# A planner's table of instruction-fetch times and a price for bank marks, with the order of a fused attention and feed-forward kernel searched anew

## The chip, the cores and the metric

The kernel runs on one core of a Trainium2 chip. The metric is the device time of one execution in microseconds (us). Five engines of the core work side by side and wait for one another by semaphores: TensorE (PE; its weight loads are listed apart as PEld), VectorE (DVE), ScalarE (ACT), GpSimd (POOL) and SyncE (SP), the last of which mostly issues transfers (DMA).

## The reference

Decayed attention without a softmax, then a feed-forward block whose gate is h cos(h). There are 8 batches of 8 heads, 576 positions and a head width of 64, so 4608 tokens of width 512; the feed-forward width is 2048.

```python
scores = scale * np.matmul(q, k.transpose(0, 1, 3, 2))
gamma = 1.0 - 2.0 ** (-5.0 - np.arange(H))
Dmat = np.where(rel >= 0, gamma[:, None, None] ** rel[None, :, :], 0.0)
x = np.matmul(scores * Dmat, v)             # then (B*S, H*D)
h = x @ w_in
out = (h * np.cos(h)) @ w_out
```

## The kernel before, in words

**Work and tiles.** Attention is computed in chunks of 64 positions with a running state of each head. A unit `(b, g)` is 256 positions of batch b (g 0 or 1) or the last 64 positions of four batches (g 2). For each unit, K, Q and V are loaded by SP, cast or weighted to bf16 (`unit`, L549 and L599), and transposed on TensorE (`tpe`, L623) or by a transposing transfer (`txb`). The scores, states and outputs are narrow matmuls on quarters of the 128x128 array (64x64 tiles); `emit_lanes` collects them in tasks whose names begin with "ses", and all run from L669. Two units make a token block of 512; there are nine. The first product of a block is either sixteen plain tiles (`mlp1`, L878) or, for blocks 4 to 8, a Strassen-like form with seven products in place of eight (`seven1`, L1007). The second product always has the seven-product form (`wino2`, L1147). These are wide matmuls on the full array.

**Banks and marks.** PSUM has eight banks of 512 columns (pool `bk`). A product that continues on a copied first product has its bank seeded by ScalarE (`seed`, L938). The bank must be "whole" for that, as its last write left it; where it isn't, `emit` (L451) first issues a mark (`mark`, L486, the matmul at L487), a matmul of ones over the bank. Places that may need one are the seeds of `seven1` and `wino2`.

**The planner.** The order isn't written by hand. `graph` builds the tasks of all engines with their durations, dependences and buffers. `prios` gives each a priority, `shift` moves priorities by a table `SHIFT` (text: an index step and a shift within some 40 us, in tens of ns), and `run` (L242) schedules: at each step it takes, over the engines, the task that can start first, among nearly equal ones that with the best priority. It keeps an instruction counter `seen` for TensorE, two for each matmul. Instructions come to TensorE in blocks of 256; `run` notes when the block k is asked for (instruction 128+256k, `asked`) and, in `pick`, delays a task that passes instruction 443+256k until that time plus `fetch(asked)` (L187). So `fetch`, a step function of the time of the run, decides how closely tasks with many small matmuls follow one another in the plan. The times exist in the plan only: the chip runs the order found. The choice of a bank prefers a whole one for a seed (L340). Where the plan has a gap on TensorE, `emit` adds filler matmuls (`warm`, L490, matmul at L493), which keep the array busy at the start.

The `SHIFT` table was found by a search outside the kernel, whose result alone stands in it.

Of the kernel before, what the change touches and what calls it, by code (L numbers as in the profile page):

```python
# [11 lines left out]
B, H, S, D = 8, 8, 576, 64  # L12
# [4 lines left out]
TB = 512  # L17
# [105 lines left out]
def lat(a, b):  # L123
    if a.dma:
        return 60
    if a.eng == b.eng:
        return 285 if a.then is b else 0 if a.eng == "pe" else 60
    return LAT[a.eng]


class Graph:
# [53 lines left out]

    @staticmethod
    def fetch(at):  # L187
        return 11500 if at < 30000 else 10000 if at < 55000 else 8500 if at < 100000 else 7200 if at < 205000 else 6200

    ENTER, LEAVE, BOND = 95, 105, 2000  # L190

    def switch(self, one, two):
# [49 lines left out]
    def run(self):  # L242
        self.reset()
        free = {e: 0.0 for e in ("pe", "act", "dve", "pool", "sp")}
        ready = {e: [] for e in free}
        seen, asked, whole = 20, {}, [False] * 8
        dma_free, port_free = 0.0, {"dve": 0.0, "pool": 0.0}
        est, order, last, mode, held = {}, [], None, "", None
# [53 lines left out]
        n = 0  # L302
        while n < len(self.tasks):
            best = None
            for e in free:
                c = pick(e)
                if c and (best is None or c[0] < best[0]):
                    best = c
            if best is None:
                rest = [(t.name, t.eng, [b.pool for b in t.allocs]) for e in ready for t in ready[e]]  # L310
                keep = {p: [b and [(t.name, t.eng) for t in b.tasks if t.start is None] for b in h] for p, h in self.holder.items()}
                raise RuntimeError(f"the scheduler is stuck: {self.pools} {free} {[x for x in rest if x[0][:3] == 'ses']} {rest[:12]} {keep}")
            s, t = best
            e = t.eng
            if e == "pe":
                s = max(s, free[e] + self.switch(mode, t.name))
            gap = s - free["pe"]
            ready[e].remove(t)
            t.start, t.order = s, n
            n += 1  # L320
            free[e] = s + t.dur
            if t.port:
                port_free[e] = s + t.dur
                if e == "dve":
                    last = t
                elif last and last.start > s - self.SINCE:
                    t.parts[0][4]["push"] = last
            if e == "pe":
                mode = t.name
                held = t.then or (held if t is not held else None)  # L330
                if gap > 400 and s < 40000:
                    seen += 2 * max(1, self.fill(gap, s - gap))
                k = (seen + t.count - 128) // 256
                if k >= 0 and k not in asked:
                    asked[k] = s + t.dur * max(0, 128 + 256 * k - seen) / max(1, t.count)
                seen += t.count
            for b in t.allocs:
                pool = self.pools[b.pool]
                ok = [i for i, f in enumerate(pool) if f is not None and f <= s + 1e-6]
                i = min(ok, key=lambda i: (b is t.seed and not whole[i], pool[i]))  # L340
                b.slot, pool[i] = i, None
                if b.pool in self.fifo:
                    self.fifo[b.pool].remove(b)
                self.holder[b.pool][i] = b
            for b, kind in t.marks:
                whole[b.slot] = kind == 1 or (kind == 2 and whole[b.slot])
            done = s + t.dur
            if t.dma is not None:
                dma_free = max(dma_free, s + (2400 if e == "pool" and s > dma_free - 700 else 1700 if e == "pool" else 1150)) + t.dma
                done = dma_free + t.tail  # L350
            for b in t.bufs:
                b.left -= 1
                b.free = max(b.free, done + (230 if e == "pe" else 170))
                if not b.left:
                    self.pools[b.pool][b.slot] = b.free
                    self.holder[b.pool][b.slot] = None
            order.append(t)
            for o in t.succ:
                end = next(x for d, x in o.deps if d is t)
                est[o] = max(est[o], (done if t.dma is not None else s + end) + lat(t, o))  # L360
                o.wait -= 1
                if not o.wait:
                    ready[o.eng].append(o)
# [5 lines left out]
class Kernel:  # L369
# [10 lines left out]
    SLABS = ((0, 'q', 0, 100), (2, 'q', 1, 101), (1, 'k', 1, 102), (3, 'k', 1, 103))  # L380
    NEXT = 2
    SHIFT = (
        "##]*#U*#u2KO$#U$D))#U=]p,)L(_5$%*'nZCce/`;)4\\)Xd/WH)]-&oG&uL/zM&`<&;.(:u$x`+m8&zq%p=0cl$ew'r&$,>/)d"
        "&na,1S)*j).F&d-&#U/#U&kW&0')wp/#g)4)%/@'5k&dv%a)$Uw$b[)b88h;(lP(pQ,|KC|K2cs)td)k|5h@%DG$yi0['*ZW&Yz"
        "*GB(\\R$jz)|K)`V0_P,{7*]n'm]1Z9(ur$D;&`t&u-&WT(o<$?.)mE)9K)CE&|C&'e$,1&1o%+Y)^*&W|%m#&|='G3)x*$[H$f0"
        "-cf*m&&;c$d_%eK)]{${q%SE;Hf$|5'[j$cR*wK'tE%pM$s7%s3$w{$v0*|K'(Z$i7.|K)sB$xQ%yv*2B$dp)rW$|K3w|*#U)$a"
        "C*#$gy%x?'x/&{P%pr'{[(j^+S]$|H%a{*aI5(c).<3-I-[h&,b%x^;m/&[j)hD&ge&$r,]E,p/$uY&h2&wT%r%%{J%s+$`q$|K"
        ",tT$&l*;q(BJ$D-%wI/)Q'>R'B,*;I%E#&Gn'J]+<O&>?7,;0Z['8^'tz*@2)8f%92$2u&q,'uc%,)&9-+5Q'9h$?#$NK$9f'?%"
        "$L/%#U$7m'Z=6|K$yB*b'3wp*Be'^k%l?&jB'Y*%CJ%eP&_9-_H&W.'tr'cc((u(a7*gs&s{)II$ss&e7$79%<,'8/%f9'\\d&,I"
        "$;7%0C(Hg+c{(v]&fG%bT.m-4(g&*t%&f(+{'#U%%D./G&)m%^&'d|-6O$<A'Ka&i?-W^%e7$aD$gZ%g('i`']x+aG,Wc"  # L390
    )
    GATE = 'k'
    TXENG = ("pool", "dve", "pool", "dve")
# [105 lines left out]
    def constants(self):  # L499
# [29 lines left out]
        for kind, ny, run in ((2, 2, 64), (4, 1, 32), (1, 1, 64)):  # L529
            n = 64 * ny * ny  # L530
            for dst, up, name in ((self.TR[kind], 0, "tr"), (self.TB[kind], 1, "tb")):
                for y in range(ny):
                    dims = ([1, 64],) if kind == 1 else ([run, 2], [1, run])
                    P.add("pool", lambda e, dst=dst, up=up, kind=kind, ny=ny, run=run, y=y, n=n, dims=dims: e.affine_select(
                        ap(dst, n, 0, 128, 128 * y, *dims), ap(self.ONE, 128, 0, 128, 0, *dims),
                        pattern=[[1, 64]] if kind == 1 else [[1, 2], [2, run]], compare_op=ALU.is_ge, fill=0.0,
                        base=64 * ny * up - y, channel_multiplier=-ny), r=["one"], w=[(name, kind, y)])
            P.add("dve", lambda e, kind=kind, n=n: e.tensor_copy(
                ap(self.TR[kind], n, 64, 64, 0, [1, n]), ap(self.TB[kind], n, 64, 64, 0, [1, n])),
                r=[("tb", kind, y) for y in range(ny)], w=[("tr", kind, y) for y in range(ny)])  # L540
# [787 lines left out]
```

## Time and profile before

| | us |
|---|---|
| median of 3 runs (lowest to highest) | 284.23 (283.28 to 284.56) |
| profiled execution, its own time | 286.41 |
| its span, first to last instruction | 284.6 |
| TensorE busy / DVE / ACT / POOL | 274.5 / 221.7 / 178.5 / 152.3 |
| mean granted TensorE clock | 0.994 |

The span is what the trace shows; the profiled execution's own time has 1.8 us around it. Shares of busy time are means over stages with different limits: the first 26 us wait for loads and weights, after that TensorE runs nearly without a break. Rows of the profile give a line of the code, the engine, the operation and the tiles by their names (`bk` is a bank, `xt` the attention's output, `gt` the gated product, `natk` and `natv` cast inputs, `tw` and `wout` second weights); in square brackets stands idle time before a row and what ended it.

### The profile page before, as it was taken

Reading aid. Unit: us, or ns where it says so; the run is one execution under the profiler, and the core shown is the slowest. Engines: PE = TensorE matmul, PEld = TensorE weight load, DVE = VectorE, ACT = ScalarE, POOL = GpSimd, SP = SyncE. Lnnn points to the kernel's source line nnn. Section 1 sums busy time; section 2 is a strip of 40 time slices with the busy share of each in tenths; the row PEclk is TensorE's granted clock in tenths of the full one; section 3 lists DMA queues with packets and bytes.
Section 4 is the critical chain, followed back from the end, with each engine's and each line's share of the span. In section 5 each row is a group of like instructions: output and inputs, shape, how many; then the busy total and the mean of one; then the engine's idle time right before and its main releaser. Section 6 shows DMA issues by size and latency. Waiting matters only on the chain.

```text
span 284.6 us, 9704 instructions
## 1 busy us (share of the span) xinstructions
PE 274.5 (96%) x4092; PEld 216.9 (76%) x4092; DVE 221.7 (78%) x384; ACT 178.5 (63%) x361; POOL 152.3 (54%) x172
## 2 busy tenths in 40 slices
PE   7799999998899999999999999999999999999995
PEld 2465688887685465578888888888888888888885
DVE  4667989989745796979969988689679946967763
ACT  5356685365326855764467877897577657978620
POOL 5452970587081528437496958974697133434410
PEclk9999999999799999999999999999999999999999
DMA  7999999899999989899989998978984102200044
GB/s 196 266 222 280 245 190 257 220 193 245 203 276 191 227 146 220 180 186 255 264 135 234 240 215 195 188 221 188 162 205 41 74 3 76 76 0 2 1 150 147
DMA packets 122731, 49.91 MB, mean 175 GB/s; under 512 B 84800, under 2 KB 118592, under 8 KB 122688
## 3 DMA queue, kind: packets, MB, share of 16 engines
q1 hardware_dynamic: 118176, 44.84, 71.3%
q0 software_dynamic: 4224, 4.19, 9.1%
q8 instruction: 32, 0.52, 0.8%
q10 hardware_dynamic: 288, 0.26, 0.3%
q14 instruction: 11, 0.09, 0.1%
HBM read 36.70 MB, written 9.44 MB: 162 GB/s over the span
## 4 chain that ended last, share of the span: by engine, by line
PE 90%; DMA 6%; issue 1%; POOL 1%; DVE 1%; ACT 0%; SPq 0%; DVEq 0%; POOLq 0%
PE bk L1147 40%; PE bk L1007 22%; PE bk L878 19%; PE bk L669 9%; DMA win<-in_moe_w_in_dram 3%; DMA stgv<-in_v_dram 2%; POOL natv L599 1%; PE bk L623 1%; DVE gt L890 0%; SPq L559 0%; PE bk L487 0%; ACT cb L887 0%; ACT qt L548 0%; DVE os L549 0%; DVEq L84 0%
## 5 line engine op out<-in xcount | busy, mean ns | idle before, releaser
L996 POOL TENSOR_TENSOR gt<-sq,cb 128x512 bf16<-128x512 f32 x40 | 46.1, 1160 | 40.6 <-DVE s L1084 14.6
L878 PE MATMUL bk<-xt,win 128*128 128x256 bf16 (+1 forms) x352 | 60.3, 321 | 1.0 <-DMA win<-in_moe_w_in_dram 0.5
L890 DVE TENSOR_TENSOR gt<-bk,cb 128x256 bf16<-128x256 f32 (+1 forms) x88 | 46.6, 542 | 14.5 <-ACT cb L887 11.1
L599 POOL TENSOR_TENSOR natv<-stgv,ia 128x512 bf16<-128x512 f32 x36 | 37.3, 1043 | 28.3 <-DVE s L1084 7.4
L887 ACT ACTIVATE cb<-bk 128x256 bf16<-128x256 f32 (+1 forms) x88 | 41.8, 482 | 16.9 <-PE bk L878 14.8
L878 PEld LDWEIGHTS bk<-xt,win 128*128 128x128 bf16 x352 | 33.0, 98 | 19.8 <-ACT cb L887 0.6
L599 POOL TENSOR_TENSOR qnat<-stgq,wq 128x512 bf16<-128x512 f32 x32 | 33.1, 1052 | 25.8 <-DMA stgq<-in_q_dram 9.7
L1147 PE MATMUL bk<-tw,s 128*128 128x256 bf16 x288 | 37.3, 280 | 0.0
L996 DVE TENSOR_TENSOR gt<-bk,cb 128x512 bf16<-128x512 f32 x40 | 27.1, 685 | 12.2 <-ACT cb L992 12.2
L1147 PE MATMUL bk<-wout,gt 128*128 128x256 bf16 x288 | 36.3, 273 | 0.0
L1147 PE MATMUL bk<-wout,s 128*128 128x256 bf16 x288 | 35.4, 273 | 0.0
L713 DVE TENSOR_TENSOR pt<-bk,tr 128x512 bf16<-128x512 f32 x48 | 30.8, 682 | 4.8 <-PE bk L669 4.8
L1007 PE MATMUL bk<-xt,win 128*128 128x256 bf16 x240 | 34.4, 273 | 0.0
L990 DVE TENSOR_TENSOR sq<-bk,sq 128x512 f32<-128x512 f32 x40 | 27.1, 684 | 8.0 <-PE bk L1007 5.5
L1147 PEld LDWEIGHTS bk<-tw,s 128*128 128x128 bf16 x288 | 28.7, 100 | 4.7 <-ACT bk L938 0.3
L549 POOL CAST natk<-stgk 128x512 bf16<-128x512 f32 x34 | 20.9, 627 | 19.6 <-DMA stgk<-in_k_dram 15.6
L992 ACT ACTIVATE cb<-bk 128x512 bf16<-128x512 f32 x40 | 23.4, 598 | 12.0 <-PE bk L1007 10.6
L1147 PEld LDWEIGHTS bk<-wout,gt 128*128 128x128 bf16 x288 | 27.8, 98 | 3.9
L1147 PEld LDWEIGHTS bk<-wout,s 128*128 128x128 bf16 x288 | 27.8, 98 | 3.7
L992 ACT ACTIVATE cb<-sq 128x512 bf16<-128x512 f32 x40 | 24.9, 630 | 7.9 <-DVE sq L990 7.1
L1007 PEld LDWEIGHTS bk<-xt,win 128*128 128x128 bf16 x240 | 23.2, 98 | 3.0
L548 ACT ACTIVATE sq<-bk 128x512 f32<-128x512 f32 x40 | 23.8, 598 | 2.0 <-PE bk L1007 2.0
(82 smaller groups left out, 415.2 us busy)
## 6 DMA issues: line engine op xcount, KB each, us to landing
stgq<-in_q_dram SPq DMA_DIRECT2D x16, 512.0 KB, 5.5
out_dram<-os SPq DMA_DIRECT2D x16, 512.0 KB, 3.9
stgk<-in_k_dram SPq DMA_DIRECT2D x20, 256.0 KB, 5.3
stgv<-in_v_dram SPq DMA_DIRECT2D x20, 256.0 KB, 5.5
stgk<-in_k_dram SPq DMA_DIRECT2D x6, 512.0 KB, 7.4
stgv<-in_v_dram SPq DMA_DIRECT2D x6, 512.0 KB, 8.1
win<-in_moe_w_in_dram POOLq DMA_DIRECT2D x4, 512.0 KB, 8.6
wout<-in_moe_w_out_dram POOLq DMA_DIRECT2D x4, 512.0 KB, 9.3
```

Source lines behind the costliest of these rows:

```text
L548: return self.one(eng, dur, lambda e: e.activation(dst(), src(), AF.Copy), r=r, w=w, **kw)
L599: self.one(eng, 610 if eng == "dve" else 1030, lambda e, out=out, inp=inp, tab=tab, col=col, hs=hs: e.tensor_tensor(out(), inp(), ap(tab, ...
L669: return lambda e: e.matmul(out(), lhs(), rhs(), start=start, stop=True, skip_group_check=True)
L713: self.one("dve", 610, lambda e, r=r, b=b, pt=pt: e.tensor_tensor(ap(self.at(pt), 1024, 0, 128, 512 * r, [64 * ny * ny, 8 // ny // ny], [1 ...
L878: inst = e.matmul(ap(self.at(bk), 512, 0, 128, 0, [1, n]), ap(self.WIN, 4 * DFF, 0, 128, c * DFF + 128 * f, [1, 128]), ap(self.at(xt), 204 ...
L887: self.one("act", n - 15, lambda e: e.activation(ap(self.at(cb), TB, 0, 128, 0, [1, n]), ap(self.at(bk), 512, 0, 128, 0, [1, n]), AF.Sin, ...
L890: self.one("dve", 75 + n / 0.96, lambda e: e.tensor_tensor(ap(self.at(gt), NF * TB, 0, 128, f * TB + 256 * h0, [1, n]), ap(self.at(bk), 51 ...
L990: self.one("dve", 610, lambda e: e.tensor_tensor(half(src), self.at(bank).ap(), half(src), ALU.add), r=[(bank,)], w=four(src))
L992: self.one("act", 530 if name else 490, lambda e: e.activation(self.at(cb).ap(), ap(self.at(src), size, 0, 128, 0, [1, 512]), AF.Sin, bias ...
L996: self.one(eng, 1120 if name else 610, lambda e: e.tensor_tensor(ap(self.at(gt), NF * TB, 0, 128, (8 * n + 2 * g) * TB + 256 * h, [TB, 2], ...
L1007: inst = e.matmul(ap(self.at(bank), 512, 0, 128, 256 * f, [1, 256]), l(c, f), rr(c), stop=True, skip_group_check=True, start=(first and f ...
L1147: inst = e.matmul(place(bank, tt), l(f, tt), rr(f), stop=True, skip_group_check=True, start=(first and f == 0 and tt < len(bank)))
```

## The change

`fetch` reads its steps from a table of seven stretches. A mark now takes 213 ns of the task that needs it in the plan (`MARK`), on TensorE's free time, on the task's end and on its successors' starts, and counts two instructions. With these the table of shifts was searched anew: 288 entries in place of 262, of which four are the same. Graph, tasks, durations of tasks and buffers are as before, and so is the code that issues them.

```diff
     @staticmethod
     def fetch(at):
-        return 11500 if at < 30000 else 10000 if at < 55000 else 8500 if at < 100000 else 7200 if at < 205000 else 6200
-
+        return next(f for end, f in Graph.FETCHES if at < end)
+
+    FETCHES = ((30000, 11500), (55000, 9500), (68000, 10200), (104000, 7800), (118000, 13000), (205000, 8800), (1e9, 6500))
+    MARK = 213
     ENTER, LEAVE, BOND = 95, 105, 2000
...
+            mark = 0
             for b in t.allocs:
                 pool = self.pools[b.pool]
                 ok = [i for i, f in enumerate(pool) if f is not None and f <= s + 1e-6]
                 i = min(ok, key=lambda i: (b is t.seed and not whole[i], pool[i]))
+                if b is t.seed and not whole[i]:
+                    mark, seen = self.MARK, seen + 2
                 b.slot, pool[i] = i, None
...
-            done = s + t.dur
+            free[e] += mark
+            done = s + t.dur + mark
...
-                est[o] = max(est[o], (done if t.dma is not None else s + end) + lat(t, o))
+                est[o] = max(est[o], (done if t.dma is not None else s + mark + end) + lat(t, o))
...
     SHIFT = (
-        "##]*#U*#u2KO$#U$D))#U=]p,)L(_5$%*'nZCce/`;)4\\)Xd/WH)]-&oG&uL/zM&`<&;.(:u$x`+m8&zq%p=0cl$ew'r&$,>/)d"
...
+        "##U*#U*#j2=I$#U$u3'|8%#U%$|;pm,D^(v)5n[$aq$EF'm)$hC$h,$)Q(b-$t9*x6Dp8)zE&|K&|K/rO&|K*su%|K)s|%qF&_U"
...
```

The steps side by side, by the time at which a block is asked for: before, 11.5 us to 30, 10.0 to 55, 8.5 to 100, 7.2 to 205 and 6.2 behind; after, 11.5 to 30, 9.5 to 55, 10.2 to 68, 7.8 to 104, 13.0 to 118, 8.8 to 205 and 6.5 behind.

More of the change, by code (lines that the diff above doesn't have):

```diff
@@ L382 @@
     SHIFT = (
-        "##]*#U*#u2KO$#U$D))#U=]p,)L(_5$%*'nZCce/`;)4\\)Xd/WH)]-&oG&uL/zM&`<&;.(:u$x`+m8&zq%p=0cl$ew'r&$,>/)d"
[L384 to L390, printed above, removed]
+        "##U*#U*#j2=I$#U$u3'|8%#U%$|;pm,D^(v)5n[$aq$EF'm)$hC$h,$)Q(b-$t9*x6Dp8)zE&|K&|K/rO&|K*su%|K)s|%qF&_U"
+        "&x'.g^$k[$cr$BS$YR$)&$5+$]=%HG'=M%/7'bZ)Yt&aA&Je&o&&/@)0{)=:)8')V-&e.&*o&]y&kT&Z'&#U)3N)L=%#U'iN)U0"
+        "%V[$@U$5w$/P$f.$\\P+]b%$>*T9'WZ%n`$_G%os$dI'y+%aR*sZ3]1'Xz*YuFu2)`oDXs%^9-(#&v$%h|'xF2K'$kt&Da'yz%eP"
+        "$|K%s;&nr&r%$c;&eA$x{.Ak,#U):r,.L&?k)ZO&1V&0U4kx&``&:U$+9(`Z&0L$#U%x4$sE&s|0b.&a.$8W$8z*iV&]_'tW,i9"
+        "*sv$qL'^I((%$lF&YQ)]K$hG$^p(80$N945u%qN*jC(mL-7i'U22B+$JD$|K.qH0zJ-FP6n1%TB'th%y(&nC$=V'g4(*,$<:*uv"
+        "'6((8\\3^/%2M%.>%5M%?b%8+/:F'3(%`l$5Q)6N*+g3&h(qn$-S&`9&4{%jP&kv&b>4_Q&I;%Ce'd[$im&du$EP$H%$|K$E[(T@"
+        "&m`%#U/vj,(,4^V&%W)i`&)[$l@(5T%HC/&F$aY-'(04q'$D']B$#a,_E):f&^4$|K&u&-{B$a[*dr/j_1d7*gU0|K*c3,li)cx"
+        "(jV'm/(il'i>&#U,Ww$K#,%/'Wp&t|)%m$)91ur$dJ$g'$4*$90$cu)^e$_m$a<$][3)H$uu)Ws/zc/1`+,h).S(:q$%-+|K%&_"
+        "&(@(<n%fW$+]&@M*1t'],'Mo$cv%nZ$_w%f)$v-(c`$lR%tY$6)*3*'^K%^,%wQ';=,{c,|K"
     )
```

## The prediction

> **What bounds the kernel now.** I read the page's busy shares first, then busy time by stretches, then TensorE's waits.
>
> ```profile
> span 284.6 us, 9704 instructions
> PE 274.5 (96%) x4092; PEld 216.9 (76%) x4092; DVE 221.7 (78%) x384; ACT 178.5 (63%) x361; POOL 152.3 (54%) x172
> ```
> ```profile
> 0.00:26.00 26.00, 21.11 (x315) 12.44 (x316) 16.18 (x44) 13.72 (x29) 11.24 (x28) 1.00 1.08 237
> 26.00:282.00 256.00, 253.40 (x3779) 204.45 (x3777) 205.25 (x340) 164.75 (x332) 141.10 (x144) 0.99 0.79 169
> 282.00:284.60 2.60, 0.00 (x0) 0.00 (x0) 0.25 (x1) 0.00 (x0) 0.00 (x0) 1.00 0.61 202
> ```
> The columns behind the length are PE, PEld, DVE, ACT, POOL, granted clock, DMA share and GB/s. TensorE is the bound: from 26 to 282 us it is busy 253.40 of 256.00 us and idle 2.60. VectorE, the next, is busy 205.25 there, 80%. The first 26 us hold 4.89 us of TensorE idle, and the last 2.60 us hold no matmul, only the last copy and store. The change removes no arithmetic, so what it can win is idle time, matmuls that do no arithmetic, and time at a lower clock. The waits of TensorE say what the idle time is:
>
> ```profile
> PE bk L669 <- issue: 2.3, 3, 1.8
> PE bk L493 <- DVE lg L519: 1.1, 1, 1.1
> PE bk L623 <- DVE qnat L599: 0.9, 2, 0.7
> PE bk L669 <- POOL natv L599: 0.7, 1, 0.7
> PE bk L878 <- DMA win<-in_moe_w_in_dram: 0.5, 1, 0.5
> ...
> PE bk L878 <- DVE gt L890: 0.2, 1, 0.2
> ```
> The columns are total us, times and the longest. "Issue" means that the engine waited for nothing the profile shows. Those are the only three waits after 26 us, and all lie inside narrow attention matmuls (L669):
>
> ```profile
> 36.40 0.22 PE L669 MATMUL bk<-natv,natk 64*64 64x64 bf16 x2 [0.20 <-issue]
> 72.14 0.31 PE L669 MATMUL bk<-natv,natk 64*64 64x64 bf16 x14 [1.82 <-issue]
> 189.09 0.26 PE L669 MATMUL bk<-qt,sba 64*64 64x64 bf16 x7 [0.23 <-issue]
> ```
> Are these the instruction fetches of the change? The queue rows and the matmul counts up to certain times (in brackets) answer it.
>
> ```profile
> q8 instruction: 32, 0.52, 0.8%
> ```
> ```profile
> 0.00:23.80 23.80, 19.09 (x304) 1.00 1.07 228
> 0.00:36.30 36.30, 31.26 (x468) 1.00 1.07 241
> 0.00:61.30 61.30, 56.16 (x801) 1.00 1.08 231
> 0.00:70.30 70.30, 65.16 (x967) 1.00 1.12 234
> 0.00:181.10 181.10, 174.14 (x2698) 0.99 1.05 218
> 0.00:189.00 189.00, 181.90 (x2867) 0.99 1.04 217
> ```
> Queue 8 moves 32 packets of 0.52/32 MB, 16 KB. TensorE has 4092 matmuls and 4092 weight loads, and 8184/32 is 256: a packet is 256 instructions. From the first wait to the second are 967-468 = 499 matmuls, 998 instructions; four blocks are 1024. From the second to the third are 1900 matmuls, 3800 instructions; fifteen blocks are 3840. The shortfalls of 26 and 40 fit semaphore instructions, which the counts leave out. So all three waits stand at block boundaries: the engine waits for its program.
>
> How long did these fetches take? The planner's rule has block k asked for when instruction 128+256k passes and needed at 443+256k. For the second wait k is 6: 1664 instructions have passed at about 61.3 us (801 matmuls are 1602, and some 60 others), so until 72.14 us the fetch took 10.8 us. The planner before assumed 8.5. For the third wait k is 21: 5504 instructions at about 181.1, so 8.0 us against 7.2 assumed. For the first k is 2: 640 at about 23.8, so 12.6 against 11.5. These are estimates, as the ask itself is not in the trace.
>
> The 1.82 us seem to cost more than themselves:
>
> ```profile
> 73.40:77.00 3.60, 3.60 (x21) 0.53 1.32 179
> 77.00:80.00 3.00, 3.00 (x30) 1.00 1.28 240
> ```
> ```profile
> PEclk9999999999799999999999999999999999999999
> ```
> Columns: length, PE busy, granted clock, DMA share, GB/s. Just after the wait the granted clock is 0.53 for 3.60 us, which loses 3.60 x 0.47 = 1.69 us. The page's 40 slices show no other between 26 and 282 us.
>
> [...] The sum below goes by the rows: the dip starts 1.3 us behind the longest wait, and I count half of it.
>
> **The change part by part.** No instruction of the computation is added or removed. Three things change: the assumed fetch times, a price for marks, and the table of priority shifts, found anew under both.
>
> *Fetch times.* The new table assumes 10.2 us where the wait of 1.82 arose (55 to 68 us), 8.8 where 0.23 arose, and an unchanged 11.5 where 0.20 arose. An order made under it keeps the narrow matmuls, which eat a block fastest, further behind the asks. If all three waits go: 1.82+0.20+0.23 = 2.25 us less. The table isn't wider than this trace everywhere: 10.8 exceeds 10.2 by 0.6, and 11.5 stays 1.1 under 12.6. A search that uses all the room it is given will leave some fetch at the edge. I charge 0.7 us for such remainders (0.6 and a tenth), between 0 and the 2.25 seen now.
>
> *The clock dip.* It costs 1.69 in the profiled execution. That execution took 286.41 us, span 284.6 and 1.8 around it; the median of the runs is 284.23, 2.18 less. A likely part of the 2.18 is that the dip isn't in every run, so I count 0.85, half of it, between 0 and 1.69.
>
> *Marks.* A mark is a 512-column matmul with no use but to set a bank's state before a seed.
>
> ```profile
> L487 PE MATMUL bk<-one 128*128 128x512 bf16 x4 | 1.5, 382 | 0.0
> ```
> ```profile
> 72.48 0.39 PE L487 MATMUL bk<-one 128*128 128x512 bf16 x1
> 72.70 1.16 PE L1147 MATMUL bk<-wout,gt 128*128 128x256 bf16 x8
> ```
> The start after the mark is 0.22 us behind the mark's, so four cost 0.88. The code has 28 places that may need one (20 in seven1, 8 in wino2). Now that they have a price, the search has a reason to use banks that are already whole. I take one fewer, 0.2 us less, between 0.9 less (none) and 0.9 more (eight), for other pressures on the banks may weigh more.
>
> *Order.* Every engine's queue is reordered, SP's and POOL's loads too. Around narrow stretches the price is small:
>
> ```profile
> 47.68 2.62 PE bk L1147 x24
> 52.84 2.73 PE bk L1147 x24
> ```
> In the chain of waits 24 wide matmuls take 2.62 us, and 2.73 behind a narrow stretch: 0.11 for a return. Two stretches more or less, each entered and left, are 0.4 either way; I take 0. Data waits after 26 us are zero now, because the other engines run ahead of TensorE with a fifth or more of their time free; a moved cast or load there is covered by this. If that cover were gone, one late transfer costs what the one at the start does, 0.5 us. The start itself is set by transfers and by the first casts; its filler matmuls are
>
> ```profile
> L493 PE MATMUL bk<-one 128*128 128x512 bf16 x24 | 8.3, 474 | 1.1 <-DVE lg L519 1.1
> ```
> 8.3 us of them, plus 4.89 idle. The first entries of the two shift tables move the same tasks (0, 7 and 14, loads) forward by 39.7 to 40.0 us both times, so the first loads come alike and I take 0, with 0.5 either way, the wait on the first weight slab. The end, 2.60 us behind the last matmul, holds a copy and a store that no order removes: 0.
>
> *Sum.* -2.25 +0.7 -0.85 -0.2 = -2.6 us. The profiled execution would go from 286.41 to 283.8, the median from 284.23 to **281.6 us**. With the ends of the terms: 284.23-2.25-0.9-0.85 = 280.2 at best without gains at the start; 283.2 where the remainders are 1.2, the dip wins nothing, and the marks stay.
>
> **The rivals.** All are counted against 284.23.
>
> *The waits move but don't go (same).* [...] For it: 12.6, 10.8 and 8.0 us were all above what the planner knew, by 0.8 to 2.3. Against it: the new table lies above two of the three old values. One wait like today's with its dip, and one mark fewer: 284.0 us.
>
> *Fetches are hidden anyway (same).* If TensorE held many blocks ahead, the waits would have another cause and stay: 284.23 less 0.2 for a mark, 284.0. The count of matmuls at the boundaries speaks against it. [...]
>
> *The dip is not bound to the wait (faster).* Then the waits go and 1.69 us at half clock stay, at some place or other: 284.23-2.25+0.7-0.2 = 282.5 us. For it: the dip begins 1.3 us after the wait has ended. Against it: TensorE was busy 26 to 70 us without one, and the first dip follows the first long wait. [...]
>
> *Two waits with dips (slower).* The new table lowers the assumed time at 30 to 55 us (10.0 to 9.5) and at 68 to 100 (8.5 to 7.8). An order that packs two narrow tasks closer there, and meets a fetch of today's 10.8 us, waits up to 3.0 us. Two long waits of today's size, each with its dip, cost 2 x (1.82+1.69) = 7.0; today's 1.82+1.69+0.43 = 3.9 go; with a mark fewer that is 284.23+7.0-3.9-0.2 = 287.1 us. It decides from the second long wait on; one alone is the case of no change. Against it: in the trace no fetch in those two stretches stopped TensorE except at 36.40, for 0.20.
>
> **How the numbers follow.** A measurement of this kernel can tell 0.5%, 1.4 us, from no change: below 282.8 is faster, above 285.65 slower. The forecast has a chance of 0.40, of which 0.38 lies below 282.8 and 0.02 above; the unbound dip 0.12 (0.09 faster, 0.03 same). Waits that move have 0.18 (0.14 same, 0.02 on each side), hidden fetches 0.05 (0.04 same, 0.01 faster), two waits with dips 0.25 (0.24 slower, 0.01 same). That makes 0.50 faster, 0.24 same, 0.26 slower. The forecast's own range, with the unbound dip, is 280.2 to 283.2. The range for 8 in 10 goes from 280.2 to 287.0: it leaves out the upper half of the slower rival, about 0.13, and some 0.05 below.
>
> **What would show it.** Right: the waits of TensorE list no issue wait above 0.6 us; the granted clock is 1.00 in every stretch from 26 to 282; L487 counts three or fewer; TensorE's idle time from 26 to the last matmul falls from 2.60 to below 1.0; the first real matmuls of L878 start as now. Wrong: issue waits of 1 us or more at other block boundaries with a clock below 1.00 behind them; or new waits on DVE, ACT or a DMA after 26 us, which would mean that the order, not the fetches, sets the time; or the fillers L493 growing in number, which would mean a later start.

## The result, and the profile after

The changed kernel takes 282.77 us (median of 22 runs, 281.81 to 284.76), the kernel before 283.95 us beside it (22 runs, 282.89 to 285.62). The ratio is 0.9959 with a 95% interval of 0.9942 to 0.9977, so 1.2 us less, where 2.6 less was forecast. The profiled execution of the changed kernel took 281.81 us, the fastest of its 22; that of the kernel before, 286.41, lay 2.5 us above its median. The pair of profiles therefore shows 4.6 us, and the medians a quarter of that. Both numbers have to be explained.

The page of the changed kernel, the lines that answer to those shown before:

```profile
span 280.1 us, 9692 instructions
PE 272.1 (97%) x4090; PEld 215.5 (77%) x4090; DVE 221.7 (79%) x384; ACT 176.8 (63%) x361; POOL 155.0 (55%) x172
PEclk9999999999999999999999999999999999999999
q8 instruction: 32, 0.52, 0.8%
```

Two matmuls fewer, the same 32 blocks of instructions, and full clock in all slices. Busy time by stretches (columns as in the prediction; the last matmul ends at 277.2 us):

```profile
0.00:26.00 26.00, 21.45 (x323) 13.23 (x324) 16.92 (x46) 13.98 (x31) 11.28 (x28) 1.00 1.08 236
26.00:277.60 251.60, 250.70 (x3769) 202.30 (x3767) 204.72 (x339) 162.80 (x331) 143.77 (x144) 1.00 0.82 172
277.60:280.10 2.50, 0.00 (x0) 0.00 (x0) 0.08 (x1) 0.00 (x0) 0.00 (x0) 1.00 0.62 204
```

Behind 26 us TensorE is idle for 251.60-250.70 = 0.90 us, against 2.60. Of these, 0.4 and 0.2 us lie behind the last matmul, which ended at 277.2 and 281.8 us. The end is as it was. The waits of TensorE, longest first:

```profile
PE bk L500 <- DVE lg L526: 1.1, 1, 1.1
PE bk L676 <- POOL natv L606: 1.0, 2, 0.7
PE bk L630 <- DVE qnat L606: 0.9, 2, 0.7
PE bk L885 <- ACT xt L555: 0.5, 1, 0.5
```

No issue wait is left in the list: all three block waits have gone in this execution. One wait of the "POOL natv" line is new, and it lies behind 26 us, in the changed kernel's timeline:

```profile
32.40 0.44 PE L676 MATMUL bk<-natv,natk 64*64 64x64 bf16 x16 [0.29 <-POOL natv L606]
```

The groups of marks and of fillers:

```profile
L500 PE MATMUL bk<-one 128*128 128x512 bf16 x24 | 8.3, 475 | 1.1 <-DVE lg L526 1.1
L494 PE MATMUL bk<-one 128*128 128x512 bf16 x2 | 0.8, 384 | 0.0
```

Two marks in place of four, and the same 24 fillers. The pair accounts for 4.6 us as 2.25 of block waits, 1.69 of half clock, 0.44 of marks and 0.2 of the rest. That is the fullest version of the forecast; the question is why the median run shows so much less of it.

### The profile page after: what moved, and what is told of

Read it like the earlier page. It is cut to its first block, busy times and chain, and to the rows that moved or that the text cites. A ratio compares the mean times of both kernels' runs of the same rounds, so it can differ in the third digit from the quotient of the medians.

```text
span 280.1 us, 9692 instructions
## 1 busy us (share of the span) xinstructions
PE 272.1 (97%) x4090; PEld 215.5 (77%) x4090; DVE 221.7 (79%) x384; ACT 176.8 (63%) x361; POOL 155.0 (55%) x172
## 4 chain that ended last, share of the span: by engine, by line
PE 89%; DMA 6%; ACT 2%; POOL 1%; SPq 1%; issue 0%; DVE 0%; POOLq 0%
PE bk L1154 40%; PE bk L1014 22%; PE bk L885 17%; PE bk L676 9%; DMA stgv<-in_v_dram 6%; POOL natv L606 1%; PE bk L500 1%; SPq L566 1%; ACT cb L894 0%; PE bk L630 0%; ACT sba L555 0%; ACT xt L555 0%; PE bk L494 0%; ACT natk L555 0%; ACT kt L555 0%
## 5 line engine op out<-in xcount | busy, mean ns | idle before, releaser
L556 POOL CAST natk<-stgk 128x512 bf16<-128x512 f32 x34 | 23.9, 712 | 27.6 <-DMA stgk<-in_k_dram 13.7
L1154 PE MATMUL bk<-tw,s 128*128 128x256 bf16 x288 | 35.6, 273 | 0.0
L1154 PEld LDWEIGHTS bk<-tw,s 128*128 128x128 bf16 x288 | 27.8, 98 | 3.7
```

The lines of the kernel that those rows point to most:

```text
L556: return self.one(eng, dur, lambda e: e.tensor_copy(dst(), src()), r=r, w=w, port=eng == "pool", **kw)
L1154: inst = e.matmul(place(bank, tt), l(f, tt), rr(f), stop=True, skip_group_check=True, start=(first and f == 0 and tt < len(bank)))
```

## Experiments

**The same two kernels again.** No edit; more traces of each, to see what a run near the median looks like.

> The kernel before, unchanged, for a second trace. Its first trace lost 2.25 us to waits for instruction blocks and 1.69 us to a clock dip, but took 2.46 us longer than the median of all runs. If late blocks set the difference from run to run (theory 1), this trace has waits at the same three places of other sizes, less than 2.25 us in sum, no clock dip where the wait near 72 us is under 1 us, and a span near 282. If the run-to-run difference has another source (theory 2), the three waits come again within 0.2 us of their size and the span differs by something else.

> The kernel before, unchanged, a third trace, to see what a typical run loses. The first two lost 2.25 us (with a dip of 1.69 behind it) and 1.98 us to waits for blocks, but both took longer than the median. Theory 1 (late blocks, varying from run to run): the wait near 72 us comes again, between 0.5 and 2 us, and if the time is within 0.5 us of the median of 284.15, the waits sum to 1 to 2 us without a dip. Theory 2: the waits are as large in a run at the median, so the longer runs come from somewhere else, the start or a late weight slab near 45 us.

> The changed kernel, unchanged, for a second trace and more runs. Its first trace had no wait for a block, and was 0.96 us shorter than the median of its runs. Theory 1: typical runs of it lose 0.5 to 1.5 us to blocks that arrive at the edge (in the first trace the fetches asked for near 24, 61, 155 and 208 us had under 0.5 us to spare), so this trace shows issue waits at one or more of those places. Theory 2: no issue wait, and the longer time comes from the start or from data. Time 282.8, ratio 0.996 in either.

> The changed kernel, unchanged, a third trace. The first two lost 0 and 0.28 us to blocks and were the shortest of their series. Theory 1: issue waits of 0.3 to 1.5 us in sum when the time is at the median of 283.0. Theory 2: no more than 0.3 us of issue waits, and the difference lies before 45 us.

> The changed kernel, unchanged, a fourth trace. Theory 3: typical runs of it lose 0.5 to 1 us to data that the kernel before does not wait for, above all to the query cast of GpSimd near 28 us, which starts when its load lands (26.7 us in the fastest trace, 27.7 in one at the median). If the load lands after 27.4 us, TensorE waits 0.3 us or more near 28 us and the time is near 282.8; if before 27, no wait and near 282.

> The changed kernel, unchanged, timed beside the three runs that follow, and a fifth trace. Ratio 0.996; block waits of 0 to 0.75 us as in the four traces so far, and 0.2 to 0.8 us of waits for GpSimd's casts between 26 and 90 us.

The kernel before took 284.38 and 284.12 us in these executions. The timeline of the first, then of the second, at the block waits behind 26 us:

```profile
36.59 0.22 PE L669 MATMUL bk<-natv,natk 64*64 64x64 bf16 x2 [0.56 <-issue]
71.92 0.31 PE L669 MATMUL bk<-natv,natk 64*64 64x64 bf16 x14 [1.42 <-issue]
```
```profile
71.63 0.31 PE L669 MATMUL bk<-natv,natk 64*64 64x64 bf16 x14 [1.55 <-issue]
```

The long wait is there each time. The dip behind it isn't; the stretches of the second execution around the wait:

```profile
70.00:74.00 4.00, 2.45 (x44) 1.97 (x37) 2.54 (x6) 1.83 (x4) 1.04 (x1) 1.00 1.01 199
74.00:80.00 6.00, 6.00 (x83) 5.17 (x82) 4.12 (x7) 1.79 (x3) 2.27 (x3) 1.00 1.29 200
```

The granted clock is 1.00 before and behind the wait. Of four traces of the old order (these two, the first one, and that without marks below, with a wait of 1.80 us) one has the dip. There it had its full price: between the 991st and the 1041st matmul the first trace loses 1.66 us on the second execution above (284.12 us, at the median), and keeps it to its last matmul, which starts 2.27 us later.

A low mean clock doesn't tell of such a dip. Of 132 runs of the kernel before that were made beside the experiments, 41 had a mean clock of 0.994 or less, as the dip of 3.60 us at 0.53 gives (1.69 us lost of 284.6), and 91 had 0.999 or 1.0; their medians are 284.29 and 284.25 us. But of the six traces of all versions with such a mean, only the first has the dip behind the wait. In the other five the half clock stands at 7 to 11 us (to 14 us in one), among the fillers at the start. One of them is the second execution of the kernel with 50 added instructions below, which up to 43 us is the kernel before:

```profile
7.40:10.80 3.40, 3.19 (x43) 2.02 (x44) 1.46 (x3) 0.60 (x1) 2.12 (x3) 0.50 1.22 261
```

Its 61st matmul starts 0.90 us later than in the execution at the median, its 341st, near 29.5 us, only 0.02 later: what the start loses is made up by then. So the runs with a low mean clock say nothing of the price of a dip at 73 us.

The changed kernel took 282.49, 282.76, 284.27 and 282.23 us in its four further profiled executions (medians of 12 runs: 283.00, ratio 0.9956, 0.9934 to 0.9979; and 282.71, ratio 0.9948, 0.9925 to 0.9970). Block waits remain in the first and the third of them, one row from each timeline:

```profile
215.19 0.22 PE L676 MATMUL bk<-qt,sba 64*64 64x64 bf16 x2 [0.28 <-issue]
```
```profile
73.99 0.44 PE L676 MATMUL bk<-natv,natk 64*64 64x64 bf16 x31 [0.75 <-issue]
```

The second of these stands at the very block that made the old kernel wait. Data waits are in every trace of the changed kernel; in the second execution (282.76 us, at the median):

```profile
28.77 0.40 PE L630 MATMUL bk<-idn,qnat 128*128 128x128 bf16 x4 [0.37 <-POOL qnat L606]
33.07 0.44 PE L676 MATMUL bk<-natv,natk 64*64 64x64 bf16 x16 [0.17 <-POOL natv L606]
87.44 0.45 PE L676 MATMUL bk<-qt,kt 64*64 64x64 bf16 x32 [0.19 <-POOL natv L606]
```

Their total behind 26 us is 0.29, 0.26, 0.73, 0.33 and 0.54 us in the five traces of the changed kernel. In the three of the kernel before, no single one reaches 0.15. The wait for `qnat` near 28 us isn't the new order's alone: two later versions of the kernel before, in which nothing is changed up to that point, have it at 0.33 us (marks left out) and 0.24 us (one task moved, second execution).

So a ledger can be made of two executions at their medians, 284.12 and 282.76 us, by adding up the distances between the starts of neighbouring matmuls behind 26 us, by kind:

| | before | after | difference |
|---|---|---|---|
| narrow matmuls, waits among them included | 26.07 | 24.52 | -1.55 |
| marks | 0.86 | 0.43 | -0.43 |
| time between wide matmuls and transposes over their cadence | 1.22 | 1.83 | +0.61 |
| same, from wide into narrow | 3.25 | 3.54 | +0.29 |
| the rest | | | -0.26 |
| start of the last matmul | 279.24 | 277.90 | -1.34 |

The two lines with a plus are those of this one execution. All of the +0.61 lies at the transposes, 0.37 of it in the wait near 28 us; between the wide matmuls of the products the two traces have the same. Its data waits, 0.73 us, are the most of the five traces. A fairer sum takes the means: the block waits behind 26 us are 1.98 and 1.55 us in the two traces of the kernel before near its median, and 0, 0.28, 0, 0.75 and 0 in the five of the changed kernel, 1.56 less. The data waits cost 0.43 more and the marks 0.43 less. That makes -1.56 us, and the times of these executions differ by 1.54 (284.25 and 282.71 in the mean).

**Blocks cut elsewhere, order kept.** Extra semaphore waits that are already satisfied stand ahead of a few wide matmuls between 43 and 58 us. They shift all later block borders and leave the order as it is: 50 in the kernel before, 24 and 102 in the changed one (other windows and counts per task).

```diff
+    PADS = ((43100, 58200, 2), )
...
+                if more:
+                    fn = self.padded(fn, more[0])
...
+                    for name in ("dve", "act", "pool"):
+                        self.e.wait_ge(sems[name], 1 + self.left)
+                return self.e.matmul(*a, **k)
```

> The kernel before, its order untouched, with 50 more semaphore instructions on TensorE that wait for long-reached values, between 43 and 58 us; they move every later block boundary 50 instructions earlier in the work. Worked out from the first trace's times of instructions and arrivals: the block that was 2.05 us late near 72 us would be 0.2 late or in time, the one near 189 us has 1.6 us to spare, and no other is later than 0.3. Theory 1: no issue wait over 0.5 us between 45 and 282 us, no clock dip, and 1 to 2 us less than the kernel before, about that of the changed kernel (ratio 0.993 to 0.997). Theory 2 (the order and the marks make the difference): ratio 1.000, or above it by the 50 instructions themselves (at most 50 x 0.05 = 2.5 us if nothing hid them).

> The kernel before with the 50 semaphore instructions of the run before_pad50, once more. That run's trace had no wait near 72 us, but 1.6 us of waits near 45 us behind a weight slab that landed 2 us later than in four other traces, before any of the added instructions. Theory 1: this was that execution's; a trace without it has a span near 281, and the median of the runs is 1 us or more below the kernel before. Theory 2 (the added instructions cost what they win, or a wait takes the place): median within 0.5 us of the kernel before again, with TensorE's waits or gaps between 43 and 60 us over 1 us.

The first time it took 283.85 us, ratio 0.9993 (0.9968 to 1.0018); repeated, 283.10, ratio 0.9955 (0.9933 to 0.9978). In the repetition no issue wait of 0.15 us or more is left behind 26 us, and one wait stands there that the kernel before never had:

```profile
86.84 0.45 PE L691 MATMUL bk<-qt,kt 64*64 64x64 bf16 x32 [0.73 <-POOL natv L621]
```

GpSimd's row shows why: its casts begin only when the load for the first of them lands.

```profile
83.73 2.05 POOL L621 TENSOR_TENSOR qnat<-stgq,wq 128x512 bf16<-128x512 f32 x2 [2.15 <-DMA stgq<-in_q_dram]
```

The first trace (285.15 us, the slowest of its twelve) also lacks the wait near 72 us, and has others, because there a slab of the second weights landed about 2 us later than in the unpadded kernel's trace at the median (the four slabs take 11.2 us from issue to landing in the median, against 9.0):

```profile
45.42 0.61 PE L504 MATMUL bk<-xt,win 128*128 128x256 bf16 x4 [1.05 <-DVE gt L912]
47.65 1.05 PE L504 MATMUL bk<-wout,gt 128*128 128x256 bf16 x8 [0.53 <-DMA wout<-in_moe_w_out_dram]
```

The wait is thus a matter of where the block border falls: moved by 50 instructions, it goes without any change of order. What it pays differs between the two series, from nothing to all of the changed kernel's gain.

> The changed kernel, order untouched, with 24 more such semaphore instructions between 43 and 54 us. From its first trace: the blocks near 71 and 214 us, now late or early by less than 0.5 us, would get 0.6 us or more to spare, and the sum of lateness falls from 1.2 to 0.4 us. Theory 1: 0.3 to 1 us less than the changed kernel (ratio 0.992 to 0.995 to the kernel before). Theory 2: the time of the changed kernel, ratio 0.996, or up to 0.5 us more.

> The changed kernel with 24 semaphore instructions near 43 to 54 us once more (the run after_pad24 was 0.5 us below the changed kernel). If the blocks at the edge near 72 and 215 us cost the changed kernel 0.3 to 0.7 us in typical runs, it is again 0.3 to 0.7 us below it, ratio 0.993 to 0.995, with no block wait in the trace. If that was chance: within 0.2 us of it.

282.49 us, ratio 0.9933 (0.9910 to 0.9956), then 283.03, ratio 0.9966 (0.9940 to 0.9991), where the changed kernel without them had 282.71 in the same series. So the first gain did not come again, and the second trace has a block wait of 0.28 us all the same, near 93 us.

> The changed kernel, order untouched, with 102 more semaphore instructions on TensorE (waits for long-reached values) between 42 and 57 us, so that every later block boundary falls 102 instructions earlier in the work. Worked out from its first two traces: the blocks needed near 109, 158 and 180 us would be 1.8 to 2.7, 0.8 to 1.0 and 1.1 us late, the sum of lateness 4.7 to 5.4 us against 1.2 to 1.4. Theory 1 (the place of the boundaries against the narrow tasks sets the time): 3 to 5 us more than the changed kernel, 286 to 288 us, ratio 1.006 to 1.014, with issue waits at those places. Theory 2 (order and marks, not boundaries): the time of the changed kernel, ratio 0.996, and up to 1 us more for the instructions.

283.77 us, ratio 0.9984 (0.9956 to 1.0013). It is about 1 us slower than the changed kernel, in the direction expected but far short of 286 to 288. Why the lateness worked out beforehand didn't come, no run shows. The one issue wait in its trace:

```profile
105.81 0.93 PE L1176 MATMUL bk<-tw,s 128*128 128x256 bf16 x7 [0.50 <-issue]
```

**The narrow task moved, alone.** In the kernel before, the output task of the fifth unit (its narrow matmuls wait near 72 us) is issued behind the next two wide tasks.

```diff
-        order = self.G.run()
+        order = self.later(self.G.run())
...
+    LATER = {"ses:2.0": 2600, "ses+2.0": 2600}
...
-                if gap > 400 and self.wb.left:
+                if gap > 400 and self.wb.left and t.start < 20000:
```

The last line keeps fillers out of the gap that the move leaves in the plan; the move near 28 to 32 us further below has it too.

> The kernel before with one move: the narrow output task of the fifth unit, which waits for the late block near 72 us, is issued behind the next two wide tasks (16 wide matmuls and a mark, 1.96 us) in place of ahead of them; nothing else changes its place on TensorE. Four traces of the kernel before show that wait at 1.42 to 1.82 us. Theory 1 (that wait is what the changed order wins): the wait is gone or under 0.3 us, and the time falls by 1.4 to 1.8 us, ratio 0.994 to 0.995. Theory 2 (the wait's removal is taken up by another wait): ratio 0.998 to 1.000, with a new wait of TensorE of 1 us or more behind 72 us.

> The kernel before_later again: the narrow task that waits near 72 us is issued behind two wide tasks. If half of the wait's 1.6 us is taken back by data that TensorE then meets unfinished: 0.5 to 1.0 us below the kernel before, ratio 0.9965 to 0.998, and data waits of 0.4 to 0.8 us between 69 and 95 us in the trace. If the first series was slow by chance: 1.3 us or more below, ratio 0.9955 or less, with no such waits.

283.71 us, ratio 0.9987 (0.9965 to 1.0009), and 283.75, ratio 0.9973 (0.9953 to 0.9994). The long wait has gone in both traces. In its place, in the first:

```profile
69.84 0.38 PE L506 MATMUL bk<-one 128*128 128x512 bf16 x1 [0.22 <-DVE gt L909]
76.11 1.92 PE L1166 MATMUL bk<-tw,s 128*128 128x256 bf16 x16 [0.15 <-DVE s L1097]
```

and one narrow stretch more, 35 in place of 34. Between the 900th and the 1100th matmul, the stretch that holds the edit, the two traces gain 0.79 and 0.78 us against the kernel before at its median. That is half of the 1.55 that went. The two waits shown are 0.37 of the other half: TensorE comes earlier to wide tasks, whose inputs VectorE has only just made. The rest isn't assigned.

**The marks left out.** The four marks aren't issued in the kernel before.

```diff
-                    self.mark(seed)
```

> The kernel before without its four marks (the seeds are then added to banks in whatever state they are in). The change has two marks in place of four. If each mark takes TensorE 0.22 us as in the trace: 0.88 us less, ratio 0.997. If the marks lie in time in which TensorE would wait for the copied seed or a block anyway: 0 to 0.2 us less, ratio 0.999 to 1.000.

283.42 us, ratio 0.9985 (0.9961 to 1.0010), 0.66 us below the kernel before by the medians. The interval holds no change, so this is a sign and not a size. Its long wait, and the stretch behind it:

```profile
72.51 0.31 PE L668 MATMUL bk<-natv,natk 64*64 64x64 bf16 x13 [1.80 <-issue]
```
```profile
74.00:80.00 6.00, 6.00 (x83) 5.17 (x82) 4.34 (x8) 2.40 (x5) 1.61 (x3) 1.00 1.30 200
```

**Both together.** The old order with the one task moved and no marks.

> The same move, and the four marks left out as well (seeds are added to banks in whatever state they are in). If the late block and the marks are what the change wins, and both are paid in the time by what the separate runs showed (0.7 for the wait, 0.5 for the marks): 1.0 to 1.4 us below the kernel before, ratio 0.995 to 0.9965, the time of the changed kernel. If the new order wins something else of its own: 0.7 us or less below.

283.09 us, ratio 0.9949 (0.9927 to 0.9971). The changed kernel has 0.9948 to 0.9959. The old order without these two things is as fast as the new one, so a gain of this size needs nothing else from the new order. It doesn't show that the change wins by the same parts: here all four marks are gone, in the changed kernel two.

**Edges of the changed kernel.** Two attempts on what it still waits for. One sets the five transposes and three narrow tasks of 28 to 32 us one wide task later; the other shortens the stores of 56 to 125 us, in which time the block needed near 73 us lands.

```diff
+    LATER = (("tpe", 27800, 30000, 880), ("ses/0.1", 31000, 32000, 880), ("ses=0.1", 31000, 32500, 880))
```
```diff
+            m = 32 if j < 3 else cn
-                bass.AP(self.out, at * DM + c0, rows + [[1, cn]]),
+                bass.AP(self.out, at * DM + c0, rows + [[1, m]]),
```

> The changed kernel with one move: the five transposing tasks and the three narrow tasks of one unit near 28 to 32 us are issued one wide task (0.9 us) later, so that the cast they wait for has 0.9 us more. Theory 3: no wait near 28 us, 0.3 to 0.6 us less than the changed kernel (ratio 0.993 to 0.995 to the kernel before), unless the scores, now 0.9 us later, make TensorE wait near 35 us for their masked copies. Theory 1 alone (only blocks matter): the time of the changed kernel, 0.996.

285.64 us, ratio 1.0039 (1.0016 to 1.0062): slower than both kernels. Its timeline has four new waits in 5 us:

```profile
30.92 0.61 PE L904 MATMUL bk<-xt,win 128*128 128x256 bf16 x4 [0.52 <-DVE qt L575]
32.44 1.04 PE L904 MATMUL bk<-xt,win 128*128 128x512 bf16 x4 [0.47 <-ACT qt L574]
34.31 0.66 PE L695 MATMUL bk<-qt,kt 64*64 64x128 bf16 x32 [0.61 <-DVE kt L575]
35.52 0.61 PE L904 MATMUL bk<-xt,win 128*128 128x256 bf16 x4 [0.56 <-DVE pt L739]
```

There is also a block wait of 0.83 us near 76 us. There is no slack to spend at 28 to 36 us: what a later transpose saves at its cast, the copies behind it lose.

> The changed kernel with the stores of the first three blocks cut from 512 to 32 columns (that part of the output is not written): about 3 MB less traffic between 56 and 125 us, every instruction in its place. Theory 3 (loads that land late, by way of GpSimd's casts, take back some of the gain): the waits near 76 and 87 us go, 0.2 to 0.5 us less than the changed kernel, ratio 0.994 to 0.9955; blocks arrive sooner too, so that the edge at 72 us may go as well, up to 0.9 us less. If neither data nor blocks cost anything there: the time of the changed kernel.

283.40 us, ratio 0.9977 (0.9949 to 1.0004): no gain on the changed kernel, and the wait was there all the same:

```profile
72.78 0.44 PE L676 MATMUL bk<-natv,natk 64*64 64x64 bf16 x31 [0.75 <-issue]
```

With fewer stored bytes the other transfers moved too, and the block landed at 71.3 us (70.7 in the execution of 282.49 us without this wait, 72.6 in that of 284.27 us with it). The run doesn't tell what sets a fetch's length.

**Prices without the new order.** The new `fetch` and `MARK` with the old `SHIFT` table.

> One part alone: the new table of fetch times and the price of marks, with the shifts of before, which were searched under the old table. If the table itself keeps narrow work off the late blocks whatever the order: no wait near 72 us, ratio 0.994 to 0.998. If shifts fit only the table they were searched under: the order falls apart into one with data waits of 2 to 10 us on TensorE, ratio 1.01 to 1.03, and block waits may still be there.

288.75 us (4 runs), ratio 1.0172 (1.0135 to 1.0209). There are no block waits either, but five marks, and data waits such as these:

```profile
139.09 0.61 PE L1013 MATMUL bk<-xs,tx 128*128 128x256 bf16 x4 [1.70 <-DVE pt L719]
...
197.40 1.05 PE L1153 MATMUL bk<-tw,s 128*128 128x256 bf16 x8 [0.35 <-DVE s L1084]
220.91 0.45 PE L675 MATMUL bk<-qt,kt 64*64 64x64 bf16 x32 [0.63 <-DVE gt L1002]
```

By the same ledger its last matmul starts 5.26 us behind that of the kernel before at the median, and about 5 us of it are time between wide matmuls and transposes and into narrow matmuls over their cadence. Waits for data, behind 26 us, are 3.6 us of this trace. With the prices this order has no block wait left; but under a shift table found with other prices it loses three times the long block wait. The new search was needed for the gain.

## Why the prediction was right and wrong

**What held.** The mechanism did. TensorE waits for blocks of its program; moving the border or the narrow task takes the long wait away; fewer marks are a part of the rest. Of the signs named, these came: no issue wait above 0.6 us in four of five traces (0.75 in the other), full clock from 26 us to the last matmul in all five, two marks, fillers unchanged, and in the first trace 0.90 us idle in place of 2.60 and the first real matmul at 13.92 us against 14.00 (14.0 to 15.5 in the other four). A sign of being wrong came too, in small: new data waits behind 26 us in every trace, two of them on VectorE (0.26 and 0.33 us), the others on GpSimd. The net of the first two terms, -2.25 +0.7 = -1.55, comes out almost exactly, but partly by luck: near its median the kernel before had 1.55 and 1.98 us of such waits, not 2.25, and the changed kernel kept 0.21 in the mean, not 0.7.

**The clock dip, -0.85, failed.** It should have been 0. The price was read rightly, 1.66 us in that execution. But the forecast explained the 2.18 us by which the execution was slow with the dip's absence from other runs, and then took half of the dip off the median all the same, which by that reasoning didn't hold it. In three further traces of the old order with waits of 1.42 to 1.80 us there is no dip behind the wait. The rival "the dip is not bound to the wait" is nearer to this, and its 282.5 us is 0.3 below the result, though in it the dip stayed to cost its 1.69. Why the dip followed the wait in one trace stays open: behind the wait of 1.82 us the granted clock read 0.53 over 3.60 us, and behind those of 1.42, 1.55 and 1.80 us it read 1.00 from 74 to 80 us.

**Order and data waits, taken at 0, failed.** "The other engines run ahead of TensorE with a fifth or more of their time free" was read from a mean over 256 us. Where TensorE comes earlier, near 28 to 34 and 87 us in the changed kernel and 70 to 76 us in the old order with the task moved, it was false: GpSimd's casts wait there for loads, and VectorE delivers just in time. The five traces of the changed kernel have 0.26 to 0.73 us of data waits for it, 0.43 in the mean; the ledger's +0.90 is the dearest of them. The old order with the wait removed shows the same: half of 1.55 does not arrive near 70 to 76 us, and 0.73 is lost in another execution near 87. The bound beside that zero, 0.5 us for one late transfer, was of the right size for one wait and was counted for none.

**Marks, -0.2, was too small.** Two went, not one: -0.43 in the ledger.

Together: -1.56 for the blocks, 0 for the dip, +0.43 for data and -0.43 for marks give -1.56, where the medians of three series differ by 1.18, 1.15 and 1.48 us. Without the dip the forecast would have been -1.75. The step that failed most was thus to read one execution, 2.5 us above the median, as the state of the kernel and then to halve its oddest part; the data waits put at nothing come next.

**The other rivals.** The waits didn't move as a whole: what remains is 0 to 0.75 us, 0.75 at the old block near 74 us and 0.28 at one near 215 us that had not waited before. With fewer stored bytes the block near 73 us landed at 71.3 us, between its 70.7 and 72.6 in two executions of the changed kernel. "Fetches are hidden anyway" fell, since moving nothing but the border takes the wait of 1.42 to 1.82 us near 72 us away. Two long waits with dips occurred in no trace.

**What stays open.** The changed kernel's runs spread by 3 us (281.81 to 284.76), more than the change. The traces differ in when loads and blocks land, and in the clock at the start: in nine of the twenty a filler near 8 us takes 0.63 us in place of 0.38, and the first product's first matmul starts at 14.5 to 15.5 us, not at 13.9 to 14.1. In the old order this is made up by 30 us, within 0.2 us in four traces of four; in the slowest trace of the changed kernel (284.27 us, start at 15.45 us) it may not be. What sets these differences wasn't found. The share of each single data wait rests on one or two executions, and the block border moved by 50 instructions paid in one series of two. No version tried beats the changed kernel by more than the scatter between its own series.

## What to carry to other kernels

A wait on the bounding engine was worth at most its length in the typical runs here, and only as far as the next input is early: before counting its removal, look at how long the inputs of the next few tasks have been ready at that place, not at the other engines' mean busy share. Take two or three traces near the median before giving a price to something that one execution shows, and look where in time a low clock lies before comparing runs by their mean clock. Prices in a planner and the order found under them belong together; one without the other can lose more than either wins.

## What the runs showed of the hardware

- In the traces looked at, the issue waits of 0.2 us and more inside TensorE's narrow work, on the changed and the unchanged kernel, stand at one place in its instruction count. With matmuls, weight loads and semaphore instructions counted, these are about numbers 961, 1985, 5825 and 6593 (within two), each about 193 more than a multiple of 256. In the first trace the packets of these blocks on queue 8 landed at 35.03, 70.53 and 187.63 us, and TensorE went on at 36.40, 72.14 and 189.09 us, 1.37 to 1.61 us later.
- A wait of 1.4 to 1.8 us on TensorE was followed by half clock (0.53 over 3.60 us) in one trace of four, and cost 1.66 us there.
- Nine of twenty traces have half speed near 8 us, by the length of a filler matmul (0.63 us in place of 0.38). In five of them the granted clock reads 0.50 there; in the other four it reads 1.00 though the matmuls are as slow (in the second trace of the kernel before, 0.63 us at 8.53 us and a clock of 1.00 over the first 10 us).
- Fifty extra satisfied semaphore waits on TensorE moved the block borders, and in one of two series cost nothing that shows: 283.10 us against 284.27 for the kernel before in the same series.
